# First-phase transfers of an RWKV-and-MoE kernel moved between SyncE's and ScalarE's queues, and a VectorE sign step folded into ScalarE's scaling

## The chip, the cores and the metric

The kernel runs on one core of a Trainium2 chip. The metric is the device time of one execution in microseconds (us). The engines are PE (TensorE), DVE (VectorE), ACT (ScalarE), POOL (GpSimd) and SP (SyncE); SP issues transfers and computes nothing. A transfer is issued by an instruction that stands in an engine's own program, so an engine that issues one does it in turn with its other work.

## What is computed

Two parts follow each other. The first is a recurrence over 768 steps for 32 heads (4 batches of 8), each with a 40x40 state:

```
for t in range(S):
    y[:, :, t] = einsum('bhd,bhde->bhe', r_t, state)
    Sa = einsum('bhde,bhe->bhd', state, a_t)
    state = state * w_t[:, :, None, :] - einsum('bhd,bhe->bhde', Sa, b_t) + einsum('bhd,bhe->bhde', v_t, k_t)
```

The second takes y as a 3072x320 matrix x: `h = x @ w_in`, then g = 0 for h <= -1, h for h >= 1 and (h+1)^2/4 between, then `g @ w_out`, with 2048 hidden columns. w_in and w_out come as float64; the kernel reads them as pairs of 32-bit words and makes float32 pairs of them.

## The kernel before

The 768 steps are cut into chunks of 32 (NC = 24); four chunks make a set s of 128 steps (NS = 6). For each set there is a preparation in three stages. "rows" multiplies decays along time and writes k, P, a and b rows to a scratch tensor in HBM, `scr[s]`. "ab" forms 32x32 products a.b per head and chunk and writes them to `abd[s]`. "inv" loads them as `lw` (`invert`, L311), inverts 128 small triangular matrices by 31 pairs of multiply (L326) and subtract (L332), and writes them to `ttd[s]`. For sets 2 to 5 this is spread between the steps of the recurrence. Sets 0 and 1 have a form of their own in the first 85 us, the first phase: `early_load` (L143) loads w, a, b and k of a set in four transfers of 640 KB; `early_products` (L149) works on DVE and POOL; `early_turn` (L177) turns a and b by PE transposes, four to a PSUM tile, and ACT copies each tile out in two pieces (L185); `early_ab` (L190) multiplies on PE, ACT copies the product into `ea` (L206), and SP stores it in eight transfers (L208). For set 0 the inversion runs on DVE, and in its middle stand the turns of `ahead` (L786): the rows of chunk 0, loaded by `load_ti` into `ti`, are transposed on DVE (L420, L423, L425) for head half 0 after 18 pairs and for head half 1 after 22. `scores` (L427) then multiplies on PE, ACT copies (L445) and POOL masks (L447).

`copy_rv` (L120) copies r and v rows of a chunk from HBM into `scr`; `early_store` (L213) stores the 640 KB of a chunk's prepared rows into `scr` (L215). `load_cg` (L390) loads pieces of `scr` (L398, L401) and of `ttd` (L409) into `cg`. Everything but a few POOL transfers is issued by SP, in the order of the program.

The recurrence is `chain` (L449): for each chunk and each half of the heads five stages of PE products with DVE and ACT between them, L463, L473, L480 and L484, L491, L498 and L503, L520, L523, L529. Its first product needs `ttd`. Between the stages stands the preparation of the weights, `weights` (L619), 28 jobs, about one for each `step`: load a block (`load_`, L651) into a lent buffer; ACT scales the high word as float32 by 2^-112 (L679); DVE mends the sign step with a multiply and a minimum (`sign`, L681 to L685); DVE shifts the low word (L714) and joins the two (L716); ACT rounds to the high part (L692), POOL subtracts for the low part (L693). 12 jobs are 512 columns wide, 16 are 320. Four jobs at the most hold a buffer until POOL is done.

From about 300 us the MoE products (`moe`, L564) fill PE beside the recurrence.

The instructions of each engine run in the order in which the program records them. The transfers of SP and ACT share eight completion semaphores, DMAHW0 to DMAHW7, given out in turn over both engines; before a transfer is issued it waits until the transfer that had the same semaphore last has landed.

Of the kernel before, what the change touches and what calls it, by code (L numbers as in the profile page):

```python
# [9 lines left out]
F32 = mybir.dt.float32  # L10
# [4 lines left out]
AF = mybir.ActivationFunctionType  # L15
ALU = mybir.AluOpType
# [33 lines left out]
def rwkv_moe_kernel(ctx: ExitStack, tc: tile.TileContext, r, k, v, w, a, b, w_in, w_out, ident_d, mask_d, out):  # L50
    nc = tc.nc
# [65 lines left out]
                ident[rows].unsqueeze(1).broadcast_to([D, 8, D]),  # L117
            )

    def copy_rv(s, part, c):  # L120

        x, o = ((r, O_R), (v, O_V))[part]
        nc.sync.dma_start(
            scr4[s][c, :, :, o : o + D], x.rearrange("b h (n t) e -> (b h) n t e", t=L)[:, 4 * s + c]
        )

# [14 lines left out]
    early_rows = {}  # L141

    def early_load(s):  # L143
        for x, n in zip(early_in[s], "wabk"):
            nc.sync.dma_start(x, srcs[n][:, 4 * s : 4 * s + 4])
            if s == 0 and n == "a":
                nc.sync.dma_start(eye, ident_d)

    def early_products(s):  # L149

        wl, al, bl, kl = early_in[s]
        R = early_out[s]
        kt, P, at, bt = (R[:, :, D * i : D * i + D] for i in range(4))
        rec = arena.rearrange("p (t e) -> p t e", e=D)
        seg = lambda x: x.rearrange("p (s t) e -> p s t e", t=8)
        Ps, ws, rs = seg(P), seg(wl), seg(rec)
        nc.vector.tensor_copy(Ps[:, 1:, 0], ws[:, 1:, 0])
        nc.vector.tensor_scalar(out=P[:, 0], in0=wl[:, 0], scalar1=-1.0, scalar2=None, op0=ALU.mult)
        for t in range(1, 8):
            nc.vector.tensor_mul(Ps[:, :, t], Ps[:, :, t - 1], ws[:, :, t])  # L160
        for i in range(1, 4):
            nc.vector.tensor_mul(Ps[:, i], Ps[:, i], Ps[:, i - 1, 7:8].broadcast_to([128, 8, D]))
        nc.gpsimd.tensor_scalar(out=at[:, 0], in0=al[:, 0], scalar1=-1.0, scalar2=None, op0=ALU.mult)
        for i in range(4):
            ts_ = slice(max(8 * i, 1), 8 * i + 8)
            nc.gpsimd.tensor_mul(at[:, ts_], al[:, ts_], P[:, max(8 * i, 1) - 1 : 8 * i + 7])
        nc.vector.reciprocal(rs[:, :, 7], Ps[:, :, 7])
        for t in range(7, 0, -1):
            nc.vector.tensor_mul(rs[:, :, t - 1], rs[:, :, t], ws[:, :, t])
        for i in range(4):  # L170
            ts_ = slice(8 * i, 8 * i + 8)
            nc.vector.tensor_mul(bt[:, ts_], bl[:, ts_], rec[:, ts_])
        for h in range(2):
            ts_ = slice(16 * h, 16 * h + 16)
            nc.gpsimd.tensor_mul(kt[:, ts_], kl[:, ts_], rec[:, ts_])

    def early_turn(s, j, part):  # L177

        for i in range(2):
            ps = psum().rearrange("p (t n) -> p t n", n=128)  # L180
            at = 8 * part + 4 * i
            for k in range(4):
                nc.tensor.transpose(ps[0:D, k, :], early_out[s][:, at + k, 80 + 40 * j : 120 + 40 * j], eye)
            for f in range(2):
                nc.scalar.copy(  # L185
                    turned[s][j][64 * f : 64 * f + D, :, at : at + 4].rearrange("e (p c) t -> e p c t", c=4),
                    ps[0:D].rearrange("e t (p f c) -> e f p c t", f=2, c=4)[:, f],
                )
# [23 lines left out]

    def early_store(s, c):  # L213

        nc.sync.dma_start(scr4[s][c, :, :, 80:240], early_out[s][c::4])  # L215

    def prelude(s):

# [400 lines left out]
    def weights():  # L619

        jobs, last = [], {}

        def into(j):
            cs = slice(512 * j, 512 * j + 512)
            for i in range(2):  # L630
                parts = [w_in[80 * i : 80 * i + 80, cs], w_in[160 + 80 * i : 200 + 80 * i, cs]]
                jobs.append((parts, None, lambda i=i, cs=cs: (w1[:, 2 * i, cs], w1[:, 2 * i + 1, cs])))
            last[len(jobs)] = cs
            jobs.append(([w_in[200:240, cs], w_in[280:320, cs]], None, lambda cs=cs: (w1[0:80, 4, cs], w1[0:80, 5, cs])))
            for f in range(4 * j, 4 * j + 4):
                ready_in[f] = len(jobs)

        def outof(f):
            ready_at[f] = len(jobs) + 1
            jobs.append(  # L640
                ([w_out[128 * f : 128 * f + 128, :]], f // 8, lambda f=f: (w2[f // 8][:, 0, f % 8], w2[f // 8][:, 1, f % 8]))
            )

        for j in range(4):
            into(j)
            for f in range(4 * j, 4 * j + 4):
                outof(f)
        todo = list(range(len(jobs)))
        size = lambda k: (sum(x.shape[0] for x in jobs[k][0]), jobs[k][0][0].shape[1])

        def load_(queue):  # L651
            while todo:
                n = 2 * size(todo[0])[1]
                fits = [j for j, x in enumerate(room) if x[0] in lending and x[1].shape[1] >= n]
                if not fits:
                    return
                kind, buf = room.pop(fits[0])
                if buf.shape[1] > n:
                    room.append((kind, buf[:, n:]))
                i = todo.pop(0)  # L660
                sts[i] = (kind, buf[:, 0:n])
                at = 0
                for src in jobs[i][0]:
                    m = src.shape[0]
                    queue.dma_start(buf[at : at + m, 0:n], src.bitcast(I32))
                    at += m

        loader.append(load_)
        load_(nc.sync)
        yield  # L670

        scaled, signed = [0], [0]
        word = lambda k, i: pair(sts[k][1])[0 : size(k)[0], :, i]

        def scale(k):
            while scaled[0] <= min(k, len(jobs) - 1) and scaled[0] in sts:
                x = word(scaled[0], 1).bitcast(F32)
                scaled[0] += 1
                nc.scalar.mul(x, x, 2.0**-112)  # L679

        def sign(k):  # L681
            while signed[0] <= k and signed[0] < scaled[0]:
                x = word(signed[0], 1).bitcast(F32)
                signed[0] += 1
                nc.vector.scalar_tensor_tensor(out=x, in0=x, scalar=2.0**32, in1=x, op0=ALU.mult, op1=ALU.min)  # L685

        def finish(k):
            while jobs[k][1] is not None and jobs[k][1] >= len(w2):
                yield
            x = word(k, 0).bitcast(F32)  # L690
            hi, lo = jobs[k][2]()
            nc.scalar.copy(hi, x)  # L692
            nc.gpsimd.tensor_sub(lo, x, hi.bitcast(F32))  # L693
            room.append(sts.pop(k))
            converted[0] = k + 1
            if k in last:
                cs, wb = last[k], w1.bitcast(F32)
                for q in range(2):
                    nc.gpsimd.dma_start(wb[80:120, 4 + q, cs], wb[40 * q : 40 * q + 40, 4, cs])

        for k in range(len(jobs)):
            scale(k + 2)
            sign(k)
            while signed[0] <= k:
                load_(nc.sync)
                yield
                scale(k + 2)
                sign(k)
            if k:
                yield from finish(k - 1)  # L710
            load_(nc.sync)
            yield
            lo, hi = (word(k, i).bitcast(U32) for i in range(2))
            nc.vector.tensor_scalar(out=lo, in0=lo, scalar1=29, scalar2=None, op0=ALU.logical_shift_right)  # L714
            sign(k + 1)
            nc.vector.scalar_tensor_tensor(  # L716
                out=lo, in0=hi, scalar=3, in1=lo, op0=ALU.logical_shift_left, op1=ALU.bitwise_or
            )
            yield
        yield from finish(len(jobs) - 1)  # L720
        yield
# [20 lines left out]
    def step_back(key, s):  # L742
        if s < NS and done.get(key, -1) < s:
            next(back[key])

    for i in range(2):
        early_load(i)
    for f in range(2):
        nc.sync.dma_start(ident[64 * f : 64 * f + 64], ident_d[64 * f : 64 * f + 64, 64 * f : 64 * f + D])
    nc.sync.dma_start(mask, mask_d)  # L750
    for c in range(4):
        for i in range(2):
            copy_rv(0, i, c)
    pad_scr(0)
    lend = lambda n, xs: room.extend((n, x.bitcast(I32)) for x in xs)
    lend(5, [Xraw[0]])
    lend(6, [Xraw[1]])
    next(wgen)
    early_products(0)
    for j in range(2):  # L760
        for k in range(4):
            early_turn(0, j, k)
    for half in range(2):
        early_ab(0, half)
    step_back("inv", 0)
    early_products(1)
    for k in range(2):
        init_cg(k, 0)
# [158 lines left out]
```

## Time and profile before

| | us |
|---|---|
| median of 3 runs | 1005.96 |
| the runs | 1005.96, 1010.69, 1002.49 |
| the profiled execution | 1003.35 |
| its span in the profile | 1001.6 |

The profile is of one execution; 1.75 us of it lie outside the span. Its views show for each engine what ran when, what ended each idle time, and the chain of waits that ended last. "SPq" is an instruction of SP that issues a transfer. Times in a view are counted from the start of the span; a matmul's end is modelled, and an engine's busy time is not by itself a limit.

### The profile page before, as it was taken

The numbers are of one execution on the slowest core, as the hardware profiler recorded it, in microseconds if no ns is written. First come the engines' busy times: TensorE is split into PE (matmuls) and PEld (weight loads), VectorE is DVE, ScalarE is ACT, GpSimd is POOL, SyncE is SP. The second block draws the span as 40 slices with busy tenths as digits, with TensorE's granted clock in tenths as the row PEclk, the third lists the DMA queues.
The fourth block names the chain that finished last, engine by engine and source line by source line (L and its number), as shares of the span: only waits on it lengthen the run. The fifth ranks groups of instructions, "written<-read, shape, count | busy, mean of one in ns | idle before, by whom it ended". The sixth has DMA issues, their size and how long they took to land.

```text
span 1001.6 us, 34605 instructions
## 1 busy us (share of the span) xinstructions
PE 800.1 (80%) x14240; PEld 715.5 (71%) x14240; DVE 569.4 (57%) x1432; ACT 530.5 (53%) x1326; POOL 588.2 (59%) x781
## 2 busy tenths in 40 slices
PE   4523644466989977989888989878999899999995
PEld 3323533355878866788787878768898789999995
DVE  7784896664755664655735676744554344545221
ACT  5823544222645643555454555455666467667663
POOL 5122667787534798444898454897447974444432
PEclk9656555676977988998899898999999999999998
DMA  9997976644787855877556877664854535442010
GB/s 270 228 221 181 203 154 159 155 104 116 156 180 164 173 122 117 164 150 148 127 126 134 166 165 143 141 132 104 148 125 88 104 82 109 107 81 61 9 44 14
DMA packets 276862, 134.56 MB, mean 134 GB/s; under 512 B 194984, under 2 KB 266856, under 8 KB 276704
## 3 DMA queue, kind: packets, MB, share of 16 engines
q1 hardware_dynamic: 273504, 121.20, 56.8%
q0 software_dynamic: 3200, 11.14, 3.8%
q8 instruction: 112, 1.84, 0.8%
q14 instruction: 46, 0.38, 0.2%
HBM read 96.83 MB, written 33.82 MB: 130 GB/s over the span
## 4 chain that ended last, share of the span: by engine, by line
PE 41%; POOL 17%; DVE 16%; DMA 11%; issue 6%; ACT 4%; SPq 4%; POOLq 0%; DVEq 0%; ACTq 0%
PE ph L600 12%; PE po L574 6%; POOL lw L326 4%; POOL lw L332 4%; PE po L578 4%; PE p L463 4%; PE p L473 3%; PE p L491 3%; POOL cg L447 3%; POOL gl L588 2%; DMA ti<-scr 2%; DVE rec L252 2%; PE p L435 2%; DVE arena L243 2%; PE p L439 2%
## 5 line engine op out<-in xcount | busy, mean ns | idle before, releaser
L600 PE MATMUL ph<-X,w 120*128 120x256 f32 x1536 | 258.5, 305 | 26.4 <-DVE qt L613 20.3
L588 POOL TENSOR_TENSOR gl<-qt,gh 128x256 fp32r<-128x256 f32 x192 | 140.5, 732 | 228.7 <-ACT gh L587 215.4
L600 PEld LDWEIGHTS ph<-X,w 120*128 120x128 f32 x1536 | 218.9, 202 | 42.7 <-DVE qt L613 24.2
L613 DVE SCALAR_TENSOR_TENSOR qt<-qt,ph 128x256 f32<-128x256 f32 x192 | 79.9, 416 | 175.6 <-ACT qt L607 167.0
L574 PE MATMUL po<-wide,gh 128*128 128x320 f32 x768 | 161.7, 326 | 0.3 <-ACT gh L587 0.3
L587 ACT CAST gh<-qt 128x256 fp32r<-128x256 f32 x192 | 78.0, 406 | 157.1 <-DVE qt L613 156.3
L447 POOL TENSOR_TENSOR cg<-cg,mask 32x512 f32<-32x512 f32 x96 | 122.5, 1276 | 38.9 <-ACT cg L445 16.4
L578 PE MATMUL po<-wide,gl 128*128 128x320 f32 x384 | 101.5, 343 | 43.4 <-POOL gl L588 43.4
L606 ACT ACTIVATE qt<-ph,half_c 128x256 f32<-128x256 f32 x192 | 90.6, 472 | 73.0 <-POOL gl L588 65.7
L574 PEld LDWEIGHTS po<-wide,gh 128*128 128x128 f32 x768 | 122.8, 199 | 3.6 <-ACT gh L587 0.5
L578 PEld LDWEIGHTS po<-wide,gl 128*128 128x128 f32 x384 | 65.9, 198 | 51.5 <-POOL gl L588 49.1
L326 POOL TENSOR_TENSOR lw<-lw 128x31 f32<-128x31 f32 (+15 forms) x155 | 93.7, 604 | 13.9 <-DMA lw<-abd 5.2
L484 ACT ACTIVATE cg<-p 32x160 f32<-32x160 f32 x192 | 56.8, 296 | 78.7 <-DVE cg L480 50.0
L491 PE MATMUL p<-cg 128*64 128x72 f32 (+1 forms) x1536 | 71.0, 253 | 33.0 <-DVE cg L480 33.0
L491 PEld LDWEIGHTS p<-cg 128*64 128x64 f32 x1536 | 63.0, 158 | 42.3 <-ACT cg L484 33.7
L332 POOL TENSOR_TENSOR lw<-lw 128x31 f32<-128x31 f32 (+15 forms) x155 | 83.7, 540 | 8.8
L480 DVE SCALAR_TENSOR_TENSOR cg<-p,mask 32x128 f32<-32x128 f32 x192 | 55.7, 290 | 57.3 <-PE p L473 31.6
L463 PE MATMUL p<-cg 128*64 128x72 f32 x1536 | 68.5, 249 | 21.1 <-DMA cg<-ttd 20.5
L607 ACT ACTIVATE qt<-qt 128x256 f32<-128x256 f32 x192 | 80.2, 417 | 6.1
L463 PEld LDWEIGHTS p<-cg 128*64 128x64 f32 x1536 | 61.1, 154 | 28.2 <-issue 24.2
L498 DVE SCALAR_TENSOR_TENSOR cg<-p,pr 40x160 f32<-40x160 f32 x184 | 59.1, 321 | 33.5 <-PE p L491 31.6
L445 ACT COPY cg<-p 32x512 f32<-32x512 f32 x96 | 55.3, 576 | 33.4 <-PE p L439 31.9
(110 smaller groups left out, 1321.7 us busy)
## 6 DMA issues: line engine op xcount, KB each, us to landing
ti<-scr SPq DMA_DIRECT2D x96, 200.0 KB
ti<-scr SPq DMA_DIRECT2D x96, 168.0 KB
scr<-arena POOLq DMA_DIRECT2D x16, 640.0 KB, 5.6
cg<-scr SPq DMA_DIRECT2D x96, 80.0 KB
X<-Y SPq DMA_DIRECT2D x36, 160.0 KB
scr<-wide SPq DMA_DIRECT2D x8, 640.0 KB
tiab<-scr SPq DMA_DIRECT2D x32, 160.0 KB
scr<-in_r_dram SPq DMA_DIRECT2D x24, 160.0 KB
```

Source lines behind the costliest of these rows:

```text
L326: eng.tensor_mul(t3, W3[:, 0:n, j : j + 1].broadcast_to([128, n, m]), L3[:, j + 1 :, j].unsqueeze(1).broadcast_to([128, n, m]),)
L332: eng.tensor_sub(W3[:, 0:n, j + 1 :], W3[:, 0:n, j + 1 :], t3)
L447: nc.gpsimd.tensor_mul(o, o, mask[q].unsqueeze(1).unsqueeze(1).broadcast_to([32, 8, 2, 32]))
L463: nc.tensor.matmul(psv[h // 8][64 * (1 - f) : 64 * (1 - f) + 64, h // 2 % 4, 0:72], lhsT=cg[:, h, C_T : C_T + 64], rhs=cg[:, h, C_R : C_R ...
L491: nc.tensor.matmul(psv[h // 8][64 * f : 64 * f + 64, h // 2 % 4, 0:n3], lhsT=cgw[:, h * CW + C_G : h * CW + C_G + 64], rhs=cg[:, h, C_R : ...
L574: nc.tensor.matmul(pos[i], lhsT=gh[:, ts_], rhs=w2[f // 8][:, j, f % 8, :], start=f == 0 and j == 0, stop=False)
L578: nc.tensor.matmul(pos[i], lhsT=gl[:, ts_], rhs=w2[f // 8][:, 0, f % 8, :], start=False, stop=f == NF - 1)
L588: nc.gpsimd.tensor_sub(gl, gt, gh.bitcast(F32))
L600: nc.tensor.matmul(ph, lhsT=w1[:, wi, fs], rhs=Xs[g][:, xi, :], start=i == 0, stop=i == 7)
L606: nc.scalar.activation(gt, ph, AF.Relu, bias=half_c, scale=0.5)
L607: nc.scalar.activation(gt, gt, AF.Square)
L613: nc.vector.scalar_tensor_tensor(out=gt, in0=gt, scalar=1.0, in1=ph, op0=ALU.min, op1=ALU.max)
```

## The change

The change has two parts. In the first phase the transfers are given to other queues and moved in the program. The early loads of set 1 go to ACT and are recorded after the first two turns of set 0's a; the copies of r and v for chunks 1 to 3 go to ACT and stand behind the two copies into `ea`, and so do the first two weight jobs' loads; the stores of set 1's prepared rows go to ACT. In the preparation of the weights the separate sign step on DVE is gone: ACT's scaling becomes a parametric rectifier with the same scale and a slope of 2^32 for negative values. Line numbers from L120 on move by one in the changed kernel, behind L680 by five to nine less.

```diff
-    def copy_rv(s, part, c):
+    def copy_rv(s, part, c, queue=nc.sync):
...
-        nc.sync.dma_start(
+        queue.dma_start(
             scr4[s][c, :, :, o : o + D], x.rearrange("b h (n t) e -> (b h) n t e", t=L)[:, 4 * s + c]
...
     def early_load(s):
+        queue = (nc.sync, nc.scalar)[s]
         for x, n in zip(early_in[s], "wabk"):
-            nc.sync.dma_start(x, srcs[n][:, 4 * s : 4 * s + 4])
+            queue.dma_start(x, srcs[n][:, 4 * s : 4 * s + 4])
...
     def early_store(s, c):
 
-        nc.sync.dma_start(scr4[s][c, :, :, 80:240], early_out[s][c::4])
+        (nc.sync, nc.scalar)[s].dma_start(scr4[s][c, :, :, 80:240], early_out[s][c::4])
...
         loader.append(load_)
-        load_(nc.sync)
+        load_(nc.scalar)
         yield
...
-                nc.scalar.mul(x, x, 2.0**-112)
-
-        def sign(k):
-            while signed[0] <= k and signed[0] < scaled[0]:
-                x = word(signed[0], 1).bitcast(F32)
-                signed[0] += 1
-                nc.vector.scalar_tensor_tensor(out=x, in0=x, scalar=2.0**32, in1=x, op0=ALU.mult, op1=ALU.min)
+                nc.scalar.activation(x, x, AF.Prelu, scale=2.0**-112, alpha=2.0**32)
...
             scale(k + 2)
-            sign(k)
-            while signed[0] <= k:
+            while scaled[0] <= k:
                 load_(nc.sync)
                 yield
                 scale(k + 2)
-                sign(k)
...
-            sign(k + 1)
...
-    for i in range(2):
-        early_load(i)
+    early_load(0)
...
-    for c in range(4):
-        for i in range(2):
-            copy_rv(0, i, c)
+    for i in range(2):
+        copy_rv(0, i, 0)
     pad_scr(0)
     lend = lambda n, xs: room.extend((n, x.bitcast(I32)) for x in xs)
-    lend(5, [Xraw[0]])
-    lend(6, [Xraw[1]])
-    next(wgen)
     early_products(0)
     for j in range(2):
         for k in range(4):
             early_turn(0, j, k)
+            if (j, k) == (0, 1):
+                early_load(1)
     for half in range(2):
         early_ab(0, half)
     step_back("inv", 0)
+    for c in range(1, 4):
+        for i in range(2):
+            copy_rv(0, i, c, nc.scalar)
+    lend(5, [Xraw[0]])
+    lend(6, [Xraw[1]])
+    next(wgen)
     early_products(1)
```

On ACT, at the end of set 1's turns in the first phase, this stands before and then in the changed kernel; names with numbers are tiles (scr_99 is the scratch tensor of set 1), and in brackets stand the semaphores that a row waits for.

```order
L185 COPY Y<-p_609 40x64x4 [waits PE_49]
L185 COPY Y<-p_609 40x64x4
L206 COPY ea<-p_624 128x512 [waits DMAHW4_49,DMAHW3_49,DMAHW5_49,DMAHW2_49,DMAHW6_49,DMAHW1_49,DMAHW7_49,DMAHW0_49,PE_49]
L206 COPY ea<-p_696 128x512 [waits PE_49]
L101 COPY cg_85<-zero_c 128x2840 [waits Activation_49]
```

```order
L186 COPY Y<-p_609 40x64x4 [waits PE_49]
L186 COPY Y<-p_609 40x64x4
L216 DMA scr_99<-wide_90 32x32x160 [waits DMAHW7_49,DVE_49]
L216 DMA scr_99<-wide_90 32x32x160 [waits DMAHW3_49]
L216 DMA scr_99<-wide_90 32x32x160 [waits DMAHW1_49]
L216 DMA scr_99<-wide_90 32x32x160 [waits DMAHW6_49]
L207 COPY ea<-p_624 128x512 [waits PE_49]
```

The four stores of set 1's rows now stand on ACT, between its last copy of the turns and its copies into `ea`.

On SP, at the loads of chunk 0's rows for the two head halves (ti_80 and ti_81), this stands before and then in the changed kernel.

```order
L398 DMA cg_83<-scr_98 32x8x80 [waits DMAHW4_49,PE_49]
L401 DMA cg_83<-scr_98 32x8x40 [waits DMAHW5_49]
L274 DMA ti_81<-scr_98 32x8x200 [waits DMAHW6_49,Pool_49]
L274 DMA ti_81<-scr_98 32x8x168 [waits DMAHW7_49]
L274 DMA ti_81<-scr_98 32x8x200 [waits DMAHW0_49]
L274 DMA ti_81<-scr_98 32x8x168 [waits DMAHW1_49]
```

```order
L399 DMA cg_83<-scr_98 32x8x80 [waits DMAHW6_49,PE_49]
L402 DMA cg_83<-scr_98 32x8x40 [waits DMAHW7_49]
L275 DMA ti_81<-scr_98 32x8x200 [waits DMAHW0_49,Pool_49]
L275 DMA ti_81<-scr_98 32x8x168 [waits DMAHW2_49]
L275 DMA ti_81<-scr_98 32x8x200 [waits DMAHW3_49]
L275 DMA ti_81<-scr_98 32x8x168 [waits DMAHW4_49]
```

The rows stand in the same order on SP, but the semaphores now went through ACT's transfers too: the holder of DMAHW7 ahead of the second `cg_83` row of 40 columns is ACT's first store into scr_99, and that of DMAHW3 ahead of the third `ti_81` row is its second.

On DVE, in the weights' part of the first recurrence stages, this stands before and then in the changed kernel.

```order
L716 SCALAR_TENSOR_TENSOR X_94<-X_94 120x512
L420 STREAM_TRANSPOSE cg_85<-ti_80 64x8x32 x2
L480 SCALAR_TENSOR_TENSOR cg_83<-p_968,mask 32x4x32 x2
L480 SCALAR_TENSOR_TENSOR cg_83<-p_969,mask 32x4x32 x2
L714 TENSOR_SCALAR tiab<-tiab 80x512
L685 SCALAR_TENSOR_TENSOR arena<-arena 128x320
L716 SCALAR_TENSOR_TENSOR tiab<-tiab 80x512
```

```order
L708 SCALAR_TENSOR_TENSOR X_94<-X_94 120x512
L421 STREAM_TRANSPOSE cg_85<-ti_80 64x8x32 x2
L481 SCALAR_TENSOR_TENSOR cg_83<-p_965,mask 32x4x32 x2
L481 SCALAR_TENSOR_TENSOR cg_83<-p_966,mask 32x4x32 x2
L707 TENSOR_SCALAR tiab<-tiab 80x512
L708 SCALAR_TENSOR_TENSOR tiab<-tiab 80x512
L424 STREAM_TRANSPOSE ev<-ti_80 128x512
```

One instruction a job is gone from DVE, and nothing else on it moved against its neighbours.

## Rows read from the trace of the kernel before

**Rows 1.** The page's chain that ended last, shares of the span by engine.

```profile
PE 41%; POOL 17%; DVE 16%; DMA 11%; issue 6%; ACT 4%; SPq 4%; POOLq 0%; DVEq 0%; ACTq 0%
```

**Rows 2.** Busy time in stretches: stretch, its length, engines (instructions), PE clock, DMA share, GB/s.

```profile
100.00:120.00 20.00, 10.63 (x210) 9.87 (x212) 18.51 (x34) 10.07 (x23) 10.89 (x9) 0.63 0.94 195
...
300.00:1001.00 701.00, 633.39 (x11168) 571.70 (x11168) 362.94 (x973) 397.91 (x1018) 427.49 (x589) 0.94 0.55 116
```

**Rows 3.** The chain in order of time, first 85 us: start, length, what.

```profile
24.51 2.33 issue
...
31.12 2.05 DMA abd<-ea
33.18 4.01 DMA lw<-abd
...
75.96 6.54 DMA ttd<-lw
```

**Rows 4.** ACT's timeline, first phase: start, length, engine, line, operation, tiles.

```profile
11.46 10.92 ACT L185 COPY cg<-p 40x256 f32<-40x256 f32 x28 [0.21 <-PE p L183]
...
28.55 0.58 ACT L206 COPY ea<-p 128x512 f32<-128x512 f32 x1 [3.74 <-PE p L202]
29.03 5.02 ACT L101 COPY cg<-zero_c 128x2840 f32<-128x2840 f32 x2
...
43.77 6.08 ACT L185 COPY Y<-p 40x256 f32<-40x256 f32 x16
```

**Rows 5.** SP's timeline, first phase.

```profile
4.08 0.60 SPq L145 DMA_DIRECT2D ti<-in_w_dram  x1
...
47.40 3.18 SPq L274 DMA_DIRECT2D ti<-scr  x4
...
64.39 7.44 SPq L208 DMA_DIRECT2D abd<-ea  x8
71.93 3.93 SPq L274 DMA_DIRECT2D ti<-scr  x8
75.96 0.40 SPq L335 DMA_DIRECT2D ttd<-lw  x1
```

**Rows 6.** DVE's timeline, second half of the first inversion.

```profile
59.65 0.90 DVE L420 STREAM_TRANSPOSE cg<-ti 64x256 f32<-64x256 f32 x2
...
62.74 1.43 DVE L326 TENSOR_TENSOR lw<-lw 128x192 f32<-128x192 f32 x1
...
68.31 0.43 DVE L326 TENSOR_TENSOR lw<-lw 128x156 f32<-128x156 f32 x1
...
71.90 0.21 DVE L332 TENSOR_TENSOR lw<-lw 128x31 f32<-128x31 f32 x1
```

**Rows 7.** POOL's timeline beside them.

```profile
62.54 5.53 POOL L447 TENSOR_TENSOR cg<-cg,mask 32x512 f32<-32x512 f32 x4 [14.80 <-issue]
```

**Rows 8.** Landings: the page's issues (KB each, us to landing), and the chain.

```profile
scr<-arena POOLq DMA_DIRECT2D x16, 640.0 KB, 5.6
...
392.30 3.99 DMA ti<-scr
```

**Rows 9.** Line 685: its sum over 84 to 190 us, then count, ns min/median/max.

```profile
sum 106.00, DVE 22.04; mean DVE 3.67
...
L685 DVE SCALAR_TENSOR_TENSOR X<-X x9: 479/686/1783, 88.1 to 169.6; 120x512 f32<-120x512 f32 x5, 80x512 f32<-80x512 f32 x3, 128x320 f32<-128x320 f32 x1
L685 DVE SCALAR_TENSOR_TENSOR arena<-arena x8: 473/480/2260, 94.3 to 167.9; 128x320 f32<-128x320 f32 x8
```

**Rows 10.** Waits of 80 to 180 us: us in total, times, longest.

```profile
PE p L491 <- DVE cg L480: 27.7, 4, 15.8
...
DVE ss L523 <- PE p L520: 3.4, 3, 1.9
```

**Rows 11.** POOL's timeline at the jobs in bulk; ACT's scaling (line 679) in ns.

```profile
143.65 6.82 POOL L693 TENSOR_TENSOR w<-X,w 120x512 fp32r<-120x512 f32 x2
...
L679 ACT ACTIVATE arena<-arena x8: 481/509/532, 89.1 to 162.5; 128x320 f32<-128x320 f32 x8
```

More of the change, by code (lines that the diff above doesn't have):

```diff
@@ L668, in weights @@
         loader.append(load_)
-        load_(nc.sync)
+        load_(nc.scalar)
         yield
-        scaled, signed = [0], [0]
+        scaled = [0]
         word = lambda k, i: pair(sts[k][1])[0 : size(k)[0], :, i]
```

## Prediction

> **What bounds the kernel now.** I read the chain of waits first, for its shares [rows 1]: PE 41%, POOL 17%, DVE 16%, DMA 11%. No engine bounds the whole, so the change has to be judged where it stands. The table of stretches comes next [rows 2]. From 100 to 120 us DVE is busy 18.51 of 20 us while PE has 10.63, ACT 10.07 and POOL 10.89: that stage is DVE's. From 300 to 1001 us PE has 633.39 of 701 us: that one is PE's. The instructions of each engine run in program order, and the change touches nothing behind about 190 us, so a shift made before then should last to the end. Then the chain in order of time [rows 3]: the chain of the recurrence waits for the first store of `ttd`, issued at 75.96 and landed 6.54 later; ahead of it stand the inversion on DVE, the load of `lw` (4.01), the stores of `abd` (2.05), and a gap of 2.33 which the profile calls issue. The timelines of ACT, SP, DVE and POOL give what stands around these [rows 4 to 7], and the waits of 80 to 180 us tell which DVE work holds PE [rows 10].
>
> I work out two numbers: B, how much later (or earlier) the `ttd` store comes through the moved transfers, and C, what the sign step gave up on DVE is worth behind it. Both are shifts of the profiled execution, 1003.35 us; the median of the runs shown is 2.61 above it, and their spread from 1002.49 to 1010.69 is wider than what is at stake.
>
> **The moved transfers (B).** First the stretch to the inversion. ACT issues set 1's four early loads behind its eighth copy of set 0's turns. An issue of this transfer takes 0.60 on SP [rows 5], and ACT copies without a gap (28 in 10.92, [rows 4]), so its later copies, and with them `ea`, come 4 x 0.60 = 2.4 later (between 0, if PE has slack, and 3.7, at the 0.93 a longer issue of SP's takes: 3.93 for eight is the short end, 7.44 for eight the long one [rows 5]). The issue gap of 2.33 ahead of PE's products may take up some of this, since the profile names no cause that is later: 0 to -2.3, I take half, -1.2. The eighth `abd` store now waits for ACT's first copy of r, which shares its semaphore and stands behind `ea`: 0.60 + a landing of 2.05 against the 1.98 by which `abd`'s last landing started behind `ea` (31.12 less 29.13): +0.7, up to +4.2 if that copy lands as slowly as the 640 KB stores do, 5.6 [rows 8]. The `lw` load runs beside ACT's copies and weight loads: its 4.01 may stretch by 0 to 2, I take 0.5. Sum +2.4: the inversion's start goes from 37.2 (33.18 + 4.01) to 39.6.
>
> The row that weighs here is the DMA share of 0.94 at 100 to 120 us [rows 2]: where transfers overlap, the engines are full whoever issued them. The Trainium skill says the same as a rule: in "DMA: Bandwidth & Descriptors", section "Issuing engines are not separate DMA queues", transfers issued from several engines run interleaved on the same 16 DMA engines, and issuing from several saves only the sequencer's time. By that rule the move to ACT could win no landing time; the trace agrees as far as that row goes. A reader who believed the opposite would take 0 for the 0.5.
>
> Second, the wait that I think decides B. ACT's tenth transfer in this phase (the last of the four weight loads) waits on the semaphore of the `lw` load, so it is issued only when `lw` has landed, 39.6, and everything of ACT behind it starts then: zero fills (29.03 before, now about 40.1) and the copies of set 1's turns, which ended at 49.85 [rows 4]. That is a block of 49.85 - 29.03 = 20.8, nearly gapless, so it now ends at 60.9. Only behind it does ACT issue the first store of set 1's rows; issue and landing take 0.5 + 4.0 (4.0 by the load in [rows 8], 5.6 at the store's own median): 65.4. On SP a `cg_83` row waits for just that store, and behind it stand the loads of `ti_81`, which DVE needs for head half 1. Before, these four were issued from 47.40 on in 3.18 [rows 5]; now the last is issued at about 68.1 (the third also waits for ACT's second store, about the same time) and lands 3.99 later [rows 8], at 72.1.
>
> DVE wants `ti_81` after 22 pairs. That was at 59.65 [rows 6], 22.45 behind the inversion's start, so now at 39.6 + 22.45 = 62.05. It stalls some 10 us, to 72.1: the turn is 72.1 - 59.65 = 12.45 later. Part comes back: four DVE instructions ran from 62.74 to 68.31, 5.57 [rows 6], three times their usual pace (the next multiply takes 0.43), while POOL's masks took 5.53 beside them [rows 7]. At the usual pace they take about 1.75, so 3.8 is at stake, and the masks for half 0 now run in the stall. I take off half, 1.9. The inversion, which ended at 72.11 [rows 6], then ends near 82.7. SP, on its way to `ttd`, has set 1's `abd` stores (7.44) and eight `ti` loads (3.93) [rows 5] behind the same wait; it is at the `ttd` store between 82 and 84. I take 83.4, against 75.96: B = +7.4. Bounds: +1 if the three small terms cancel to that and ACT's block shrinks under the slack of 10 us; +15 if the late landings (5.6 for 4, 4.2 for 0.7, 2 for 0.5) hold and SP comes last. No row shows ACT's issues in this phase, so the end stays that wide. The `cg` loads and copies of r and v which come later are needed only by the recurrence's first chunks, behind `ttd`; if that cover were gone the price would be one landing, about 4.
>
> **The sign step (C).** It ran 28 times, 12 of 512 columns and 16 of 320, and cost DVE 22.04 from 84 to 190 us; the medians are 0.69 and 0.48 [rows 9], so 12 x 0.69 + 16 x 0.48 = 16.0 of its own, the rest being a few slow ones (up to 2.26), beside POOL. On the path counts only what stands ahead of a DVE result for which PE waits: PE waits 27.7 for L480 in four places, while DVE waits for PE only 3.4 in three [rows 10]. By the order some three stand behind L425 and ahead of L523, in one of DVE's waits; two wait for loads, and two stand at the end. That leaves 21: 9 x 0.69 + 12 x 0.48 = 12.0. Four of these, around 143 us, only keep POOL short of work (two of its subtractions fill 6.82 there, [rows 11]): -1; and when DVE is done earlier ACT or a load is late next in places: another -1. I take C = -10; bounds -4 (DMA at 0.94 in the stretch [rows 2] and POOL set the pace instead) and -16 (all of it on the path).
>
> On ACT the scaling is the same instruction with another function. No row shows this rectifier; the row of the scaling has 0.51 for 128x320 [rows 11], which I take, with 0 extra. If it took twice that, ACT would have 28 x 0.5 = 14 more in a stage where it is idle half the time [rows 2], and I would give back 3 of C; if it were quicker nothing changes, as ACT doesn't bound. The Trainium skill ("ScalarE: Activation LUTs", "What ACT_TABLE_LOAD costs") gives one element per cycle and lane for every function, by which the 0 holds; no run here shows it yet.
>
> Net: B + C = +7.4 - 10 = -2.6, so 1003.35 - 2.6 = 1000.75, rounded 1000.8.
>
> **Rivals.** (1) Slower: ACT's first store of set 1 holds SP and DVE longer than reckoned. Place: SP's `cg_83` row ahead of `ti_81`. Price: B = +15, time 1003.35 + 15 - 10 = 1008.4. It is slower than before from the point where B passes 10. For it: the long landings (5.6, [rows 8]) and SP's long issues beside full DMA engines; against it: the four places where time could come back were each taken at half or less. (2) Faster: the stall is small, because ACT's tenth transfer is issued early or its block shrinks (copies of the turns then find their products waiting), B = +1, and the masks no longer slow DVE, C = -13: 1003.35 - 12 = 991.4. For it: the terms ahead of the inversion are small and partly cancel; against it: 20.8 us of ACT's copies were gapless already [rows 4], so they hardly shrink. (3) The sign step was hidden by POOL's subtractions and full DMA engines: C = -3, B = +7.4, time 1007.8; for it the 0.94 and the 6.82, against it DVE's 18.51 of 20.
>
> **How the numbers follow.** The forecast gets 0.50, rival 1 0.15, rival 2 0.27, rival 3 0.08. About 1% (10 us) is what a measurement of this kernel can tell from no change. Rival 2 mostly lies past that, and the forecast's lower edge a little: faster by over 1% 0.30. Slower by over 1% needs B near 20, or rivals 1 and 3 together: 0.11. Within: 0.59. The range takes in rival 2 with room for a C of -16 (988) and rival 1 with the 2.6 by which a median may lie above the profiled run (1011). The likeliest case alone runs from 996 to 1005.
>
> **What would show it.** Right: ACT's last weight load waits on the `lw` load and its zero fills start near 40; SP's second `cg_83` row of 40 columns waits for a store to scr_99; DVE idles some 10 us before L421 for `ti_81`; the `ttd` store is issued at 82 to 84; from there to 190 us the same work takes about 10 less, with no sign step on DVE and 0.5 us a scaling on ACT. Wrong: DVE reaches `ti_81` without a stall, the `ttd` store comes before 78 or behind 88, or the stretch behind it shrinks by under 4.

## The result and the profile after

| | before | changed |
|---|---|---|
| median of 19 runs each, us | 1004.89 | 1011.93 |
| the profiled execution, us | 1003.35 | 1012.19 |
| its span, us | 1001.6 | 1010.4 |

The ratio of the changed kernel to the one before is 1.0066, with a 95% interval of 1.0044 to 1.0088: some 7 us slower, where 2.6 faster was forecast. 1011.93 also lies just above the range's end of 1011. One of the 19 runs of the kernel before, 1103.47, was a slow one and is not in the ratio.

The profile shows two large shifts of opposite sign. The first phase is late. This is SyncE's timeline in the changed kernel (start, length, engine, line, operation); the rows answer to [rows 5].

```profile
26.65 7.58 SPq L209 DMA_DIRECT2D abd<-ea  x8
38.19 0.35 SPq L317 DMA_DIRECT2D lw<-abd  x1
...
55.86 0.30 SPq L399 DMA_DIRECT2D cg<-scr  x1
68.91 0.30 SPq L402 DMA_DIRECT2D cg<-scr  x1
69.31 4.33 SPq L275 DMA_DIRECT2D ti<-scr  x4
...
80.59 5.42 SPq L209 DMA_DIRECT2D abd<-ea  x8
86.11 4.17 SPq L275 DMA_DIRECT2D ti<-scr  x8
90.38 0.38 SPq L336 DMA_DIRECT2D ttd<-lw  x1
```

Between 55.86 and 68.91 SyncE issues nothing: its second row of 40 columns for `cg` is held. What it waits for is on ScalarE, whose timeline follows; it answers to [rows 4].

```profile
15.53 9.14 ACT L186 COPY cg<-p 40x256 f32<-40x256 f32 x24 [1.93 <-PE p L184]
...
29.93 0.58 ACT L207 COPY ea<-p 128x512 f32<-128x512 f32 x1 [3.31 <-PE p L203]
29.93 0.64 ACTq L123 DMA_DIRECT2D scr<-in_r_dram  x1
...
36.84 8.11 ACTq L666 DMA_DIRECT2D X<-in_moe_w_in_dram  x4
45.05 5.01 ACT L101 COPY cg<-zero_c 128x2840 f32<-128x2840 f32 x2 [14.54 <-DMA X<-in_moe_w_in_dram]
...
64.04 0.69 ACTq L216 DMA_DIRECT2D scr<-wide  x1
```

The four weight loads (line 666) take 8.11, since the last of them waits until `lw` has landed; the zero fills stand 14.54 idle and start at 45.05 instead of 29.03. The store of line 216 is issued at 64.04, and the chain of waits carries on from there:

```profile
64.04 4.85 DMA scr<-wide
68.91 0.30 SPq L402
...
72.77 6.83 DMA ti<-scr
79.73 0.44 DVE cg L421
...
90.38 6.74 DMA ttd<-lw
```

64.04 + 4.85 is 68.89, the instant at which SyncE goes on. VectorE's timeline shows the stall in two pieces; its start answers to the load in [rows 3], the turn to [rows 6].

```profile
44.72 0.21 DVE L327 TENSOR_TENSOR lw<-lw 128x31 f32<-128x31 f32 x1 [11.50 <-DMA lw<-abd]
...
77.99 0.44 DVE L421 STREAM_TRANSPOSE cg<-ti 64x256 f32<-64x256 f32 x1 [10.88 <-DMA ti<-scr]
79.73 0.44 DVE L421 STREAM_TRANSPOSE cg<-ti 64x256 f32<-64x256 f32 x1 [1.31 <-DMA ti<-scr]
```

So B, the shift of the `ttd` store, is 90.38 - 75.96 = 14.4. The second shift stands behind it. Two marks frame the stretch in which the weights are prepared: the recurrence's first product on PE, and the first product of the MoE's activation on VectorE (`qt`). These rows are of PE's and VectorE's timelines, before:

```profile
84.36 2.55 PE L463 MATMUL p<-cg 128*64 128x72 f32 x32 [20.50 <-DMA cg<-ttd]
205.33 0.42 DVE L613 SCALAR_TENSOR_TENSOR qt<-qt,ph 128x256 f32<-128x256 f32 x1 [0.99 <-ACT qt L607]
```

and in the changed kernel:

```profile
99.03 2.61 PE L464 MATMUL p<-cg 128*64 128x72 f32 x32 [15.55 <-DMA cg<-ttd]
210.09 0.42 DVE L614 SCALAR_TENSOR_TENSOR qt<-qt,ph 128x256 f32<-128x256 f32 x1 [0.99 <-ACT qt L608]
```

The stretch took 205.33 - 84.36 = 120.97 before and 210.09 - 99.03 = 111.06 now: C is -9.9. The shift is +14.7 at the first mark and +4.8 at the second. In this execution another 4.0 are added behind it, in the stage that is PE's: from `qt` to the end 796.3 before (1001.6 - 205.33) and 800.3 now. From 280 to 460 us TensorE's granted clock had a mean of 0.82 of full speed, against 0.84 before.

### The profile page after: what moved, and what is told of

Its sections match the earlier page's. It is cut to its first block, busy times and chain, and to the rows that moved or that the text cites. A ratio compares the mean times of both kernels' runs of the same rounds, so it can differ in the third digit from the quotient of the medians.

```text
span 1010.4 us, 34586 instructions
## 1 busy us (share of the span) xinstructions
PE 809.5 (80%) x14240; PEld 725.2 (72%) x14240; DVE 552.0 (55%) x1404; ACT 530.2 (52%) x1326; POOL 580.9 (57%) x781
## 4 chain that ended last, share of the span: by engine, by line
PE 44%; POOL 15%; DVE 13%; DMA 11%; issue 8%; ACT 5%; SPq 3%; ACTq 0%; DVEq 0%; POOLq 0%
PE ph L601 12%; PE po L575 7%; PE po L579 4%; POOL lw L327 4%; PE p L474 4%; PE p L464 4%; PE p L492 3%; POOL lw L333 3%; DMA ti<-scr 3%; POOL cg L448 2%; POOL gl L589 2%; PE p L436 2%; DVE rec L253 2%; PE p L521 2%; PE p L530 2%
## 5 line engine op out<-in xcount | busy, mean ns | idle before, releaser
L601 PE MATMUL ph<-X,w 120*128 120x256 f32 x1536 | 262.0, 309 | 21.7 <-DVE qt L614 19.6
L601 PEld LDWEIGHTS ph<-X,w 120*128 120x128 f32 x1536 | 223.0, 206 | 37.3 <-DVE qt L614 24.8
L448 POOL TENSOR_TENSOR cg<-cg,mask 32x512 f32<-32x512 f32 x96 | 122.5, 1276 | 40.1 <-ACT cg L446 18.3
L607 ACT ACTIVATE qt<-ph,half_c 128x256 f32<-128x256 f32 x192 | 90.5, 471 | 72.1 <-POOL gl L589 63.6
L492 PEld LDWEIGHTS p<-cg 128*64 128x64 f32 x1536 | 65.1, 162 | 37.0 <-ACT cg L485 28.0
L464 PE MATMUL p<-cg 128*64 128x72 f32 x1536 | 70.8, 252 | 19.0 <-DMA cg<-ttd 15.5
L464 PEld LDWEIGHTS p<-cg 128*64 128x64 f32 x1536 | 62.7, 157 | 26.5 <-issue 22.9
```

The costliest lines, as they stand in the source:

```text
L448: nc.gpsimd.tensor_mul(o, o, mask[q].unsqueeze(1).unsqueeze(1).broadcast_to([32, 8, 2, 32]))
L464: nc.tensor.matmul(psv[h // 8][64 * (1 - f) : 64 * (1 - f) + 64, h // 2 % 4, 0:72], lhsT=cg[:, h, C_T : C_T + 64], rhs=cg[:, h, C_R : C_R ...
L492: nc.tensor.matmul(psv[h // 8][64 * f : 64 * f + 64, h // 2 % 4, 0:n3], lhsT=cgw[:, h * CW + C_G : h * CW + C_G + 64], rhs=cg[:, h, C_R : ...
L601: nc.tensor.matmul(ph, lhsT=w1[:, wi, fs], rhs=Xs[g][:, xi, :], start=i == 0, stop=i == 7)
L607: nc.scalar.activation(gt, ph, AF.Relu, bias=half_c, scale=0.5)
```

## The experiments

The theory going in (T): the first phase is late because the two queues wait for each other, and the sign step gives back some 10 that last. Rival A: most of what the sign step frees is lost again later. Rival B: the DMA engines are full, and where a transfer is issued makes no difference. All ratios are to the kernel before, on the same chip, with 95% intervals.

**The sign step alone** (transfers as before):

```diff
-                nc.scalar.mul(x, x, 2.0**-112)
-        def sign(k):
...
+                nc.scalar.activation(x, x, AF.Prelu, scale=2.0**-112, alpha=2.0**32)
...
```

> The kernel before with only the sign step folded into ScalarE's scaling; all transfers as before. Theory T (the moved transfers cost what the profile of the changed kernel shows ahead of the ttd store, 14.4 us, and the sign step gives back 10.5 by about 157 us and keeps it): about 10 us less than before, ratio 0.990, ttd store at 76 as before. Rival A (most of what the sign step frees is given back behind 275 us, where the profile of the changed kernel lost 5 us again): 4 to 6 less, ratio 0.995. Scaling on ScalarE 0.51 us for 128x320 as before under both; 0.6 or more would be a price of the rectifier that neither has.

Measured: 993.36, ratio 0.9883 (0.9851 to 0.9916). The same two marks, and ScalarE's scaling by line (ns min/median/max):

```profile
84.78 2.44 PE L463 MATMUL p<-cg 128*64 128x72 f32 x32 [21.01 <-DMA cg<-ttd]
193.21 0.42 DVE L613 SCALAR_TENSOR_TENSOR qt<-qt,ph 128x256 f32<-128x256 f32 x1 [0.99 <-ACT qt L607]
...
L679 ACT ACTIVATE arena<-arena x8: 478/496/520, 89.4 to 151.5; 128x320 f32<-128x320 f32 x8
```

The stretch is 108.4, 12.5 shorter than before, and the end keeps 11.8 of it (span 989.8 against 1001.6). Rival A falls. The rectifier costs ScalarE nothing: 496 ns against 509 in [rows 11].

**The queues alone** (the changed kernel with the sign step back on VectorE):

```diff
...
-                nc.scalar.activation(x, x, AF.Prelu, scale=2.0**-112, alpha=2.0**32)
+                nc.scalar.mul(x, x, 2.0**-112)
+        def sign(k):
...
+            sign(k + 1)
...
```

> The changed kernel with the sign step put back on VectorE; all transfers as in the change. Theory T: the ttd store at about 90, as in the changed kernel, and the whole 14 us last to the end: ratio 1.014. Rival A: the same store at 90, but the end only 11 to 12 later, ratio 1.011 to 1.012. If the store is back near 76, both are wrong about what delays it.

Measured: 1021.12, ratio 1.0154 (1.0121 to 1.0187): 15.5 us slower, with 12.2 and 18.8 as the ends of the interval. The `ttd` store in its chain of waits:

```profile
91.15 6.27 DMA ttd<-lw
```

The shift is 15.2 at the store (91.15 - 75.96) and, by the ratio, 15.5 at the end; the medians differ by 14.1 and the two profiled spans by 17.7. Within that spread nothing of the first phase is made good later. Rival A's 1.012 lies just below the interval.

**Set 1's stores back on SyncE**, else as changed:

```diff
-        (nc.sync, nc.scalar)[s].dma_start(scr4[s][c, :, :, 80:240], early_out[s][c::4])
+        nc.sync.dma_start(scr4[s][c, :, :, 80:240], early_out[s][c::4])
```

> The changed kernel with the four stores of set 1's rows back on SyncE, at their old place in its order; everything else as changed. Theory T (SyncE's loads of ti_81 wait for ScalarE's stores, which stand behind a late ScalarE): the inversion starts at 44.7 as in the changed kernel, the turn of head half 1 comes at about 67 without a stall instead of 79.7, the ttd store at about 80: 10 us less than the changed kernel, ratio to before about 0.997. Rival B (full DMA engines, not waits between queues, make the phase late): the stores land no sooner from SyncE, the turn stays at 78 to 80, ratio about 1.006.

Measured: 1006.94, ratio 0.9997 (0.9968 to 1.0027). The turn of head half 1 starts at 67.61, as T said, so B falls: from SyncE the same loads land in time. The ratio lies near T's 0.997 and clear of B's 1.006. But the `ttd` store was issued at 87.71, not 80. VectorE's timeline says why:

```profile
67.61 0.90 DVE L421 STREAM_TRANSPOSE cg<-ti 64x256 f32<-64x256 f32 x2
76.08 0.71 DVE L424 STREAM_TRANSPOSE ev<-ti 128x512 f32<-128x512 f32 x1 [7.57 <-PE p L440]
```

The next transpose overwrites `ev`, and PE's scores of head half 0 still have to read it. They stand on PE behind set 1's products (line 203), which wait for ScalarE's copies, and then through a gap of 4.22 for which the profile names no cause:

```profile
66.15 3.18 PE L203 MATMUL p<-Y,cg 40*32 40x32 f32 x208 [2.04 <-ACT Y L186]
73.55 0.81 PE L203 MATMUL p<-Y,cg 40*32 40x32 f32 x44 [4.22 <-issue]
```

With SyncE's wait gone, ScalarE's lateness reaches VectorE by a second route; the first had hidden it. T had missed that. On the other hand the `ttd` store, with SyncE in time and its last loads issued 3.7 ahead of it, landed in 2.62 instead of 6.54 [rows 3], as its chain shows:

```profile
87.71 2.62 DMA ttd<-lw
```

**The weight loads back on SyncE**, else as changed:

```diff
-        load_(nc.scalar)
+        load_(nc.sync)
```

> The changed kernel with the first two weight jobs' four loads on SyncE at the same place of the program (behind the lw load), so that no transfer of ScalarE waits for the lw load. Theory T: ScalarE's zero fills start at about 37 instead of 45.05, its first store of set 1's rows at about 56 instead of 64, and the turn of head half 1 at about 71 instead of 79.7; ttd store at about 82, ratio to before about 0.999. Rival B (full DMA engines): the turn stays within 2 us of 79.7, ratio about 1.006.

Measured: 1003.25, ratio 0.9974 (0.9948 to 0.9999). ScalarE's zero fills, and VectorE's start and stall:

```profile
38.60 5.02 ACT L101 COPY cg<-zero_c 128x2840 f32<-128x2840 f32 x2 [8.53 <-DMA scr<-in_r_dram]
...
41.77 0.21 DVE L327 TENSOR_TENSOR lw<-lw 128x31 f32<-128x31 f32 x1 [9.02 <-DMA lw<-abd]
...
72.51 0.44 DVE L421 STREAM_TRANSPOSE cg<-ti 64x256 f32<-64x256 f32 x1 [8.39 <-DMA ti<-scr]
74.44 0.44 DVE L421 STREAM_TRANSPOSE cg<-ti 64x256 f32<-64x256 f32 x1 [1.49 <-DMA ti<-scr]
```

ScalarE comes 6.5 sooner (8 were expected; its copies of r and v still hold it, now for 8.53), and the turn 5.3 sooner. The inversion starts 3 sooner too: without ScalarE's weight loads in flight `lw` landed in 3.7 instead of 6.5, although SyncE now issues the same four loads right behind it, at 38.36. The `ttd` store is issued at 85.79, where 82 was expected. B does not explain a turn that moves by 5.3.

**Both of these together**:

```diff
-        load_(nc.scalar)
+        load_(nc.sync)
...
-        (nc.sync, nc.scalar)[s].dma_start(scr4[s][c, :, :, 80:240], early_out[s][c::4])
+        nc.sync.dma_start(scr4[s][c, :, :, 80:240], early_out[s][c::4])
```

> The changed kernel with both the weight loads and set 1's stores back on SyncE; the copies of r and v for chunks 1 to 3 and the early loads stay on ScalarE. Theory T: ScalarE's zero fills at about 38 (its copies of r and v still hold it for 8 us), SyncE waits for no store; the inversion at about 42, the turn of head half 1 at about 64 to 66 with a short stall, the ttd store at 78 to 80, the first stage of the recurrence 1 to 4 us later than before, ratio 0.990 to 0.993. If the gains of the two edits don't add (a third route holds VectorE), ratio 0.997 as with either alone.

Measured: 1003.83, ratio 0.9978 (0.9954 to 1.0003): a miss for T's size; the 0.997 expected if the gains don't add lies in the interval. VectorE's wait at `ev`, and SyncE's `ttd` store:

```profile
67.56 0.71 DVE L424 STREAM_TRANSPOSE ev<-ti 128x512 f32<-128x512 f32 x1 [2.09 <-PE p L440]
...
83.27 0.39 SPq L336 DMA_DIRECT2D ttd<-lw  x1
```

The stall is nearly gone (2.09 left at `ev`) and the inversion ends at 79.1, but SyncE, with the stores again ahead of its `abd` stores and loads, reaches the `ttd` store only at 83.27. The gains of the two edits do not add: what the one frees, SyncE's own list takes. What is left against the kernel before, 7.3 at the store, lies by elimination with the copies of r and v on ScalarE and the weight loads' later place in the program, since the early loads alone turn out to be worth about 1 (below); no run moves either of the two by itself.

**Only set 1's stores on ScalarE**, on top of the sign step alone:

```diff
-        nc.sync.dma_start(scr4[s][c, :, :, 80:240], early_out[s][c::4])
+        (nc.sync, nc.scalar)[s].dma_start(scr4[s][c, :, :, 80:240], early_out[s][c::4])
```

> The kernel before with the sign step folded into ScalarE's scaling and only the four stores of set 1's rows moved to ScalarE, all else on SyncE as before. By the order of waits, SyncE's fourth early weight load now waits on the semaphore that ScalarE's first such store holds, and that store stands behind ScalarE's copies of set 1's turns. Theory T (a semaphore shared by the two queues makes SyncE wait for a late ScalarE): set 0's abd stores start only at about 56, the inversion at 68 to 70 instead of 37, the ttd store at about 104, the whole about 17 us slower than before, ratio 1.017. Rival B (the queues don't hold each other; SyncE only loses four issues): ttd store at 72 to 76, ratio 0.985 to 0.988.

Measured: 1018.91, ratio 1.0126 (1.009 to 1.0163): 12.7 us slower than before and some 24 slower than without this edit. This run shows the shared semaphore most plainly. SyncE's timeline, and ScalarE's:

```profile
23.03 30.38 SPq L665 DMA_DIRECT2D X<-in_moe_w_in_dram  x4
53.54 8.29 SPq L208 DMA_DIRECT2D abd<-ea  x8
...
48.28 0.67 ACTq L215 DMA_DIRECT2D scr<-wide  x1
```

Four loads of weights, which need nothing of set 1 and had taken 1.9 from SyncE, take 30.38; 28.7 of it is one wait, the fourth load's for a semaphore that ScalarE's first store holds. That store is issued at 48.28; SyncE goes on at 53. The inversion starts at 67.60 and the `ttd` store is issued at 102.36, within 2 us of what the order of waits had said. The end is 4 better than expected, about what the store's landing gives, 2.6 instead of 6.5 [rows 3].

**Only set 1's early loads on ScalarE**, on top of the sign step alone:

```diff
-            nc.sync.dma_start(x, srcs[n][:, 4 * s : 4 * s + 4])
+            (nc.sync, nc.scalar)[s].dma_start(x, srcs[n][:, 4 * s : 4 * s + 4])
...
-    for i in range(2):
-        early_load(i)
+    early_load(0)
...
+            if (j, k) == (0, 1):
+                early_load(1)
```

> The kernel before with the sign step folded and only set 1's four early loads moved to ScalarE, behind the second turn, as in the change. No wait of either queue is on a later transfer of the other here. Theory T: ea about 1.4 us later as in the changed kernel, inversion start 38 to 39, no stall at ti_81, ttd store 76 to 78: 0 to 2 us behind the sign step alone (ratio 0.988 to 0.991). Rival B (the early loads on ScalarE are what makes the phase late, through the DMA engines): inversion start 42 or later, ratio 0.993 or more.

Measured: 997.09, ratio 0.992 (0.9895 to 0.9946). `ea` comes 2.9 later than before, twice what was expected. The inversion starts at 39.81 and the `ttd` store is issued at 77.35, 1.0 later than with the sign step alone; there is no stall at `ti_81`. The inversion starts between the two expectations (38 to 39 under T, 42 or later under B), and the interval of the ratio takes in the ends of both. This part of the change is the small one, 1 to 4 us.

**A version that might beat both**: the sign step alone, and chunk 1's eight `ti` loads moved on SyncE from ahead of the `ttd` store to behind the loads from `ttd`:

```diff
         scores(0, hb)
-        if NC > 1:
-            load_ti(1, hb)
...
     for hb in range(2):
         load_cg(0, hb, (1,))
+    for hb in range(2):
+        load_ti(1, hb)
```

> Looked for as better than both: the kernel before with the sign step folded, and the eight loads of chunk 1's rows (ti) taken from ahead of the ttd store on SyncE to behind the loads from ttd. Theory: SyncE reaches the ttd store when VectorE is done, at about 72.2 instead of 76; the store, no longer behind 1.5 MB of loads, lands in 2.6 us as in the run with the stores on SyncE instead of 6.5; the first product of the recurrence at 77 to 78 instead of 84.4; 5 to 7 us off the run with the sign step alone, ratio 0.982 to 0.984. Rival: the eight loads land late and VectorE waits for them at the first turn of chunk 1, giving back most of it: ratio 0.986 to 0.988.

Measured: 995.21, ratio 0.989 (0.9857 to 0.9923), which the sign step alone had already. The first part of the expectation held: the store is issued at 71.98, lands in 2.62, and PE starts 8.3 sooner than with the sign step alone. Then it is lost. It isn't lost at the first turn of chunk 1, as the expected rival had it: that turn starts at 81.90 without a wait. PE's first product, VectorE's `qt`, and two stretches (length, PE, PEld, DVE, ACT, POOL, clock, DMA share):

```profile
76.51 2.49 PE L463 MATMUL p<-cg 128*64 128x72 f32 x32 [11.86 <-DMA cg<-ttd]
192.44 0.42 DVE L613 SCALAR_TENSOR_TENSOR qt<-qt,ph 128x256 f32<-128x256 f32 x1 [0.99 <-ACT qt L607]
...
100.00:120.00 20.00, 14.11 (x247) 12.54 (x244) 17.07 (x32) 10.34 (x25) 10.69 (x11) 0.50 1.07 203
120.00:145.00 25.00, 8.05 (x160) 7.09 (x160) 17.87 (x26) 11.03 (x24) 13.87 (x13) 0.50 0.93 209
```

At `qt` only 0.8 of the 8.3 is left. From 120 to 145 us VectorE is busy 17.87 of 25, against 22.39 with the sign step alone; the DMA engines are full, and the chain of waits there holds loads of `ti` that took 8.43 and 6.44 to land:

```profile
115.88 8.43 DMA ti<-scr
...
128.80 6.44 DMA ti<-scr
```

That these landings take back the gain is read from the chain; no run tests it.

## Why the prediction was wrong

**The mechanism was named; its size decided the sign.** Every wait that the prediction listed is in the profile: ScalarE's last weight load on `lw`, the zero fills behind it, SyncE's `cg` row on ScalarE's first store, VectorE's stall before `ti_81`. The mark that it set for being wrong (a `ttd` store behind 88) was passed: 90.38. What happened is rival 1, B = +15, which had a chance of 0.15. The steps that failed are three prices of transfers in the sum for B: the eighth `abd` store, the `lw` load and the `ti_81` loads.

| step | predicted | measured |
|---|---|---|
| `ea` done | 30.3 | 30.5 |
| inversion starts | 39.6 | 44.7 |
| ScalarE's zero fills start | 40.1 | 45.05 |
| its first store of set 1 has landed | 65.4 | 68.9 |
| last `ti_81` load issued | 68.1 | 72.8 |
| turn of head half 1 (its second transpose) | 72.1 | 79.7 |
| `ttd` store | 83.4 | 90.4 |

**Issues on ScalarE and the gap on PE: right in sum, in part by luck.** Four early loads at 0.61 to 0.66 each and half of the gap put `ea` within 0.2 us. But the loads stopped ScalarE's copies for 1.9, not 2.4 (the idle time in its row at 15.53), and the gap ahead of PE's products only went from 2.33 to 2.01, where 1.2 was taken off. The difference was made up by two things that the sum did not have: ScalarE's first copy came 0.6 later (10.21 instead of 9.65), and PE's products ahead of the gap took 1.86 instead of 2.47.

**The eighth `abd` store: mis-sized.** "+0.7, up to +4.2" was taken at 0.7. From the end of `ea` to the `lw` load it was 4.05 before and is 7.7 now, +3.6. The store did wait for ScalarE's first copy of r: its issue starts at 33.93, 3.4 behind `ea`, where 2.65 was reckoned. That is 0.8 of the 2.9 by which the term was too small. The other 2.1 are the store's own landing, 4.2 instead of 2.05, which the prediction left as it was without a reason. The chain of waits of the run with the weight loads on SyncE shows both, the copy's landing and the store's, ahead of `lw`:

```profile
29.48 4.21 DMA scr<-in_r_dram
33.71 4.21 DMA abd<-ea
37.97 3.71 DMA lw<-abd
```

That the total comes near the upper bound is chance, since that bound was set for a late copy alone. The runs place the delay on the copies of r and v. With them on ScalarE and the weight loads taken off, the way from `ea` to `lw` is 7.9 (run with the loads on SyncE); with the copies on SyncE early it is 3.7 (only the early loads on ScalarE).

**The `lw` load: mis-sized.** It took 6.5 (38.19 to 44.72) against 4.1 before, +2.4 where 0.5 was taken and 2 was the bound; with only the stores back on SyncE it took 7.4, and in the runs without ScalarE's weight loads in flight 3.7 to 4.1.

**The block on ScalarE: right but for 1.8.** 64.04 - 45.05 = 19.0 against 20.8, since the store was issued among the last copies rather than behind them.

**From the store's landing to the turn: mis-sized.** 10.8 passed (68.9 to 79.7), not 6.7: the last of the four `ti_81` loads was issued 3.9 behind the landing instead of 2.7, and it landed 6.83 later, not 3.99. The row taken was of a load at 392 us, [rows 8]; the two `ti` loads that the first phase of the kernel before has in its chain take 6.5 and 6.3:

```profile
42.72 6.50 DMA ti<-scr
...
49.24 6.27 DMA ti<-scr
```

**POOL's masks: right.** 1.9 was taken off, and 1.8 came back: two instructions of the inversion were slowed instead of four.

The three mis-sized terms, +2.9, +1.9 and +4.1, less the 1.8, give the 7 by which B was too small; the other differences, 0.2 to 0.7 each, nearly cancel. The first two were taken near the quiet end of their bounds and the third had no bound, though this phase is the crowded one. A stretch of the changed kernel (length, PE, PEld, DVE, ACT, POOL, clock, DMA share) that holds the `abd` stores and the `lw` load:

```profile
28.00:46.00 18.00, 5.11 (x119) 3.76 (x119) 6.26 (x12) 1.54 (x2) 3.87 (x4) 0.59 1.09 188
```

The DMA share, packet times summed over the time of 16 engines, is above 1 there; from 69 to 80 us, around the `ti_81` loads, it is 1.08. All three terms are transfers that share the engines with others. The Trainium skill's rule in "DMA: Bandwidth & Descriptors" ("Issuing engines are not separate DMA queues") bears on the same point: transfers of both queues interleave on the same engines, and the trace agrees, 6.5 for `lw` beside ScalarE's loads and 3.7 to 4.1 without them. It doesn't follow that the issuer makes no difference: the same four loads, issued by SyncE right behind `lw`, left it at 3.7 (4.1 with the stores on SyncE too). Whether that comes of the queue or of the order of the issues, no run separates.

**C: right.** -10 was forecast; -9.9 in the changed kernel and -12.5 by itself. The single terms of its sum were not measured apart. The condition that a shift pass through to the end held too, as far as the spread of the runs lets one see, in both runs that tested one part alone (11.8 of 12.5, and 14.1 to 17.7 of 15.2).

**What stays open.** The two parts alone multiply to 0.9883 x 1.0154 = 1.0035, the change measures 1.0066. The intervals overlap. The 4.0 that the changed kernel's profile lost behind `qt`, at a lower granted clock, are within what single executions differ by: that stretch, which no edit touches, took from 796.3 to 807.6 in the ten profiled executions. But the median of the changed kernel, too, lies 7 above, more than the 4.8 at `qt`, and no run settles it. By the same spread the times of the runs with the stores or the loads back on SyncE follow the shift of their `ttd` store only roughly: with the loads back the store is issued 4.6 sooner than in the changed kernel, and the time is some 9 shorter.

## What to carry to other kernels

A transfer moved to another engine's queue stays tied to the first queue: where both share completion semaphores, each later transfer may wait for whoever held its semaphore, so look up the holder of every wait before moving one, and ask how late that engine itself runs. Where transfers crowd, price a landing by the crowded rows, and when a sum hangs on three such prices, let the upper ends set the sign's chance; a landing taken as before needs a reason too. When a wait on a late engine is removed, look for the second route by which its lateness comes through.

## What the runs showed of the hardware

The store of `ttd`, 512 KB, landed in 2.62 when no loads had been issued just ahead of it (set 1's stores on SyncE; `ti` loads behind the store) and in 6.2 to 6.7 right behind 1.5 MB of loads. A multiply or subtract of the inversion that took 0.3 to 0.5 took 1.3 to 1.4 while POOL's masks ran beside it, in the changed kernel as before [rows 6, 7]; VectorE's timeline in the changed kernel, and POOL's:

```profile
84.15 0.42 DVE L327 TENSOR_TENSOR lw<-lw 128x156 f32<-128x156 f32 x1
84.61 1.27 DVE L333 TENSOR_TENSOR lw<-lw 128x156 f32<-128x156 f32 x1
...
84.17 2.85 POOL L448 TENSOR_TENSOR cg<-cg,mask 32x512 f32<-32x512 f32 x2 [3.77 <-ACT cg L446]
```

The parametric rectifier costs ScalarE what the plain scaling did, 0.50 us for 128x320, which agrees with the Trainium skill's one rate for every function ("ScalarE: Activation LUTs", "What ACT_TABLE_LOAD costs").
